# A list scheduler's order: late big loads and independent marked moves in a forgetting-attention and gated-MLP kernel

## The chip, the cores and the metric

One core of one Trainium2 chip. The metric is the device time of one execution in microseconds (us). Besides TensorE (PE), VectorE (DVE), ScalarE (ACT) and GpSimd (POOL), SyncE (SP) issues all of this kernel's DMAs, in one queue, in order.

## The reference

Eight batches of eight heads, 576 positions, head size 64, then one MLP over all 4608 tokens:

```python
scores = (q @ k.T) / sqrt(64)
cum    = cumsum(log(clip(f, 1e-4, 1)))
scores = where(causal, -1e9, scores + cum[:, None] - cum[None, :])
attn   = softmax(scores);  o = attn @ v            # 8 x 8 x 576 x 64
x      = o as [4608, 512]
h      = x @ w_in                                  # 512 -> 2048
g      = h * tanh(softplus(h))                     # Mish
out    = g @ w_out                                 # 2048 -> 512
```

## The kernel before, in words

All operands are split into two float16 halves (high and low), so a product is three matmuls. Two heads are a pair; there are 32 pairs. For a pair `load_qk` (L1047) brings q and k in one transfer of 576 KB into one of two buffers `qk32`; `prep` (L1060) sums their squares on ACT (`junk<-qk`), picks a scale on DVE (`qt`), splits them into `hl`, and issues DMAs into `ST1`: two small copies of cumulated-decay rows from DRAM (`st<-cumd`, 6.8 KB, L1087) and the heads (`st<-hl`); `prep2` (L1094) fills `ST2`. Pairs 1 and 3 use `xa1` in place of `hl`. `load_v` (L980) brings a batch's v in four transfers of 288 KB; `amax_v` sums their squares (`junk<-v`). Then come scores, maxima on DVE (`highest`, a custom instruction that leaves `mn`), exponents on ACT (`st<-b`, `more_e<-b`), their halves `hb`, a transpose by DMA (`pt<-hb`), the products with v (`b<-vv,pt`), normalizing (`x<-b,rr`) and its halves `xp`, transposed into `xa`. The first five pairs go an older way.

The MLP takes 512 tokens at a time (a chunk, 9 in all): products with `w_in` (`b<-xa,wall`), Mish on ACT (`me<-b`), a scaling into halves `gh` and `gl`, products with `w_out` (`b<-gh,wall`, `b<-gl,wall`). Mish and the exponent need different ACT tables, so a change between them is an `ACT_TABLE_LOAD`. Weights come as 32 transfers of 512 KB, are shifted and masked by DVE (`wall<-wall`), summed, scaled and split. The attention of later batches is woven into the MLP of earlier chunks. Chunks 7 and 8 use a scheme with fewer products for part of `w_in`, at the cost of DVE work (sums and differences).

No instruction is issued where the code stands. `Program.choose` (L188) records each operation with its reads and writes, and, where there are several, its possible engines; `deps` (L305) makes dependencies of them; `schedule` (L365) runs `forward` (L478), a list scheduler with a model of the engines and of one DMA queue, and `backward`, which ranks the operations anew, ten times, and keeps one of the ten orders; `emit` (L327, the calls at L333) issues every instruction in that order. The engine of an operation with a choice is picked in `forward` too. The waits that the chip obeys come from the buffers that an instruction really touches, not from this model. `warmed` (L335) puts in matmuls of no use (`b<-idm,idh`) where the model sees PE idle early on.

Two things order transfers among themselves in the model alone. While `nc.mark` is set, each recorded operation also writes an invented region of that name; while `nc.gate` is set, it reads one. `prep` marks the two row copies of pairs 0 to 3 as `rows0` to `rows3`; `load_weights`, the loads of pairs 2 and 3, and the first `load_v` are gated by `rows0`, the next `load_v` by `rows2`. And in `forward` a transfer is taken to have landed at a time worked out from its size:

```python
hw = max(t, hw) + cost[0]
clock[q] = t + 50
dma = max(dma, hw + 650) + cost[1]
end, own = dma + 930 + MARGIN["sync"], 0.0
```

`cost[1]` is the size in bytes over 290, in ns (L272), and t is the model's own time in ns.

Of the kernel before, what the change touches and what calls it, by code (L numbers as in the profile page):

```python
# [27 lines left out]
S = 576  # L28
D = 64
# [100 lines left out]
BACK = 4000  # L130
LOOK = dict(zip(('tensor', 'vector', 'scalar', 'gpsimd', 'sync'), (float(x) for x in ("0", "0", "0", "0", "0",))))
PRIO = 200
MARGIN = dict(tensor=100,vector=100,scalar=100,gpsimd=0,sync=300)
DRAWS = 4
WORK, LAGS, MOVES = 0.02, 50.0, 300.0
F32COL = 8.3
MSW = 97.0
# [23 lines left out]
class Program:  # L161
# [26 lines left out]
    def choose(self, *ways):  # L188

        r, w, opts = [], [], []  # L190
        for way in ways:
            total, port = 0.0, False
            for eng, method, a, kw in way:
                aps = [(k, x) for k, x in list(enumerate(a)) + list(kw.items()) if hasattr(x, "tensor")]
                w += [z for k, x in aps if k in ("out", "accum_out", 0) for z in self.region(x)]
                r += [z for k, x in aps if k not in ("out", "accum_out", 0) for z in self.region(x)]
                if eng == "scalar":
                    (r if method == "activation" else w).append(("table", 0, 1, 0, 1))
                if eng == "tensor":

                    w.append((w[0][0] + "/pe", 0, 1, 0, 1))
                port |= self.shared(eng, method, aps)
                cost = self.cost(eng, method, kw, aps)
                if isinstance(cost, tuple) and total:

                    total = (total[0] + 8, total[1] + cost[1], 0)
                else:
                    total = cost if isinstance(cost, tuple) else total + cost + (80 if total else 0)
            opts.append((eng, way, total, port))
        if self.gate:  # L210
            r.append((self.gate, 0, 1, 0, 1))
        if self.mark:
            w.append((self.mark, 0, 1, 0, 1))
        key = len(self.ops)
        if self.rank is not None:
            key, self.rank[1] = self.rank[0] + self.rank[1], self.rank[1] + self.rank[2]
        self.ops.append((opts, r, w, key))
        self.leads.append(self.lead)
        self.forms.append(self.form(*ways[0][0]) if ways[0][0][0] == "tensor" else None)
        func = ways[0][0][3].get("func") if ways[0][0][0] == "scalar" and len(ways) == 1 else None  # L220
        self.sets.append("mish" if func == AF.Mish else "exp" if func == AF.Exp else None)
        if self.sets[-1] and self.phase is not None:
            n = len(self.sets)
            w.append((f"phase{self.phase}", 0, 1, n, n + 1))
            r.append((f"phase{self.phase - 1}", 0, 1, 0, 1 << 30))

        self.banks.append({
            x.tensor.name for _, _, a, kw in ways[0] for x in list(a) + list(kw.values())
            if hasattr(x, "tensor") and x.space == PSUM})
# [248 lines left out]
    def forward(self, deps, succ, rank):  # L478
# [43 lines left out]
        while len(order) < n:  # L522
            clock["sync"] = max(clock["sync"], hw, dma - BACK)
            best = None
            for q in self.NAMES:
                r, c = ripe[q], coming[q]
# [4 lines left out]
                if r or c:  # L531
                    t = clock[q] if r else max(clock[q], c[0][0])
# [59 lines left out]
            if way[0][1].startswith("dma_start"):  # L592
                hw = max(t, hw) + cost[0]
                clock[q] = t + 50
                dma = max(dma, hw + 650) + cost[1]
                end, own = dma + 930 + MARGIN["sync"], 0.0
            else:
                if q == "tensor":
                    cols, weight, h = cost
# [84 lines left out]
def attn_moe(ctx: ExitStack, tc: tile.TileContext, qk, v, f, w_in, w_out, out):  # L684
# [91 lines left out]
    def flat(t):  # L776
        return t[0:BH].rearrange("p j t s -> p (j t s)")

    tmp = [flat(ST2[i]).bitcast(F32)[:, S * j : S * (j + 1)] for i in (1, 0) for j in range(2)]
    ft = tmp[0]  # L780

    def decay():
        _, on, cm, r1 = tmp
        nc.vector.memset(on, 1.0)
        nc.vector.tensor_scalar(out=ft, in0=ft, scalar1=1e-4, scalar2=1.0, op0=ALU.max, op1=ALU.min)
        nc.scalar.activation(out=ft, in_=ft, func=AF.Ln)
        nc.scalar.preload_act_table_set("exp_and_others")
        nc.vector.tensor_tensor_scan(
            out=cm, data0=on, data1=ft, initial=0.0, op0=ALU.mult, op1=ALU.add)
        c = flat(ST2[1])[:, 0 : 3 * S].rearrange("p (r s) -> p r s", r=3)  # L790
        nc.vector.tensor_scalar(out=c[:, 0], in0=cm, scalar1=8.0, scalar2=None, op0=ALU.mult)
        nc.vector.scalar_tensor_tensor(
            out=r1, in0=cm, scalar=8.0, in1=c[:, 0], op0=ALU.mult, op1=ALU.subtract)
        nc.vector.tensor_copy(out=c[:, 1], in_=r1)
        nc.vector.tensor_tensor(out=c[:, 2], in0=r1, in1=c[:, 1], op=ALU.subtract)
        nc.mark = "sums"
        for h in (slice(0, H), slice(H, BH)):
            nc.mark = None if h.start else "sums"
            nc.sync.dma_start(out=cumd[h], in_=c[h])
        nc.mark = None  # L800
# [259 lines left out]
    def prep(g):  # L1060
# [23 lines left out]
        h0 = b * H + 2 * p  # L1084
        nc.mark = f"rows{g}" if g < NSEL else None
        for t in range(2):
            nc.sync.dma_start(out=ST1[i][D + 3 * t : D + 3 * t + 3, :, t], in_=cumd[h0 : h0 + 2].rearrange("h r s -> r h s"))  # L1087
        nc.mark = None
        for j in range(2):
# [907 lines left out]
```

## Time and profile before

| | |
|---|---|
| median of 3 runs | 1014.1 us (1013.09 to 1015.46) |
| the profiled execution, its own time | 1014.29 us |
| its span on the core | 1012.6 us |
| mean granted TensorE clock | 0.993 |
| PE, DVE, ACT busy, share of the span | 97%, 72%, 72% |
| matmul records, ACT table loads | 7663, 71 |

Nearly all instructions have one line, L333 (the one that issues), so groups are told by the names of the tiles. A PE that is shown busy can still be short of work inside, since matmuls overlap: a matmul of 512 columns is shown with 0.38 us and the next starts 0.22 us after it. "Idle before" is the time in which the engine had nothing running, with what ended it.

### The profile page before, as it was taken

The page shows a single profiled execution, that of the slowest core. Times are in us where ns is not written, and L with a number is a line of the kernel's source. Part 1 is how long each engine was busy: PE and PEld are TensorE (multiplying, and loading weights), DVE is VectorE, ACT ScalarE, POOL GpSimd, SP SyncE. Part 2 cuts the span into 40 slices and gives each one's busy share as a digit, 9 for nine tenths or more (in the row PEclk, how much of TensorE's full clock was granted, in tenths as well). Part 3 has the DMA queues.
Part 4 walks back from the last instruction along what each step waited for, and adds up shares of the span by engine and source line. Part 5 has one row for each costly group of instructions (what it writes and reads, how often), then busy time and mean ns, then how long its engine had stood idle before and what let it go on. Part 6 is the DMA issues. An engine that isn't in the chain of part 4 may idle for free.

```text
span 1012.6 us, 20652 instructions
## 1 busy us (share of the span) xinstructions
PE 978.1 (97%) x7663; PEld 544.1 (54%) x7663; DVE 731.1 (72%) x2002; ACT 728.9 (72%) x1421; POOL 10.4 (1%) x65
## 2 busy tenths in 40 slices
PE   4999899998999999999999999999999999999998
PEld 4788445544554554555455555455555555656664
DVE  7999999986677776776666766776766669953432
ACT  6668999978778777777778877787886665524323
POOL 2000000000000000000000000000000000000000
PEclk8999999999999999999999999999999999999999
DMA  6999974779777857687868766786775432001001
GB/s 198 324 266 244 262 169 108 154 173 187 158 145 160 173 127 153 136 180 145 142 141 179 148 146 142 170 158 115 138 152 112 70 75 72 4 1 42 1 1 42
DMA packets 256446, 139.57 MB, mean 138 GB/s; under 512 B 226650, under 2 KB 227034, under 8 KB 256346
## 3 DMA queue, kind: packets, MB, share of 16 engines
q1 hardware_dynamic: 256346, 138.26, 61.7%
q8 instruction: 60, 0.98, 0.4%
q14 instruction: 40, 0.33, 0.1%
HBM read 45.68 MB, written 9.66 MB: 55 GB/s over the span
## 4 chain that ended last, share of the span: by engine, by line
PE 65%; DVE 16%; ACT 7%; DMA 6%; issue 3%; SPq 1%; POOL 0%; DVEq 0%; ACTq 0%; POOLq 0%
PE b L333 65%; DVE wall L333 3%; DVE b L333 2%; DMA pt<-hb 2%; DMA st<-hl 2%; SPq L333 1%; ACT junk L333 1%; DVE hl L333 1%; DVE hb L333 1%; ACT st L333 1%; ACT hb L333 1%; DMA out_dram<-ot 1%; DVE gl L333 1%; DVE x L333 1%; ACT more_e L333 1%
## 5 line engine op out<-in xcount | busy, mean ns | idle before, releaser
L333 PEld LDWEIGHTS <-wall 128*128 128x128 f16 x3372 | 322.3, 98 | 357.9 <-issue 24.0
L333 PE MATMUL b<-gh,wall 128*128 128x512 f16 x1152 | 366.5, 380 | 0.0
L333 PE MATMUL b<-xa,wall 128*128 128x512 f16 (+1 forms) x1602 | 345.0, 366 | 8.3 <-ACT me L333 4.6
L333 PE MATMUL b<-gl,wall 128*128 128x512 f16 x576 | 218.2, 379 | 0.6 <-DVE gl L333 0.6
L333 PE MATMUL b<-st 70*128 70x512 f16 (+11 forms) x918 | 139.1, 285 | 13.7 <-DMA st<-cumd 6.9
L333 DVE SCALAR_TENSOR_TENSOR gl<-me,gsc,gh 128x512 f16<-128x512 f32 x144 | 106.3, 748 | 32.6 <-ACT gh L333 31.7
L333 ACT ACTIVATE me<-b,cinv 128x512 f32<-128x512 f32 (+1 forms) x130 | 85.0, 660 | 56.6 <-PE b L333 55.7
L333 PEld LDWEIGHTS <-st 70*128 70x128 f16 (+3 forms) x1110 | 87.3, 102 | 63.6 <-issue 18.7
L333 PE MATMUL b<-vv,pt 128*128 128x65 f16 (+5 forms) x2548 | 111.7, 203 | 1.1 <-DMA pt<-hb 0.7
L333 DVE CUSTOM_DVE_ANT_0 b<-b,mskw 128x256 f32<-128x256 f32 (+2 forms) x162 | 91.6, 567 | 9.9 <-PE b L333 8.8
L333 ACT ACT_TABLE_LOAD x70 | 89.8, 1283 | 1.2
L333 PEld LDWEIGHTS <-pt 128*128 128x128 f16 (+1 forms) x2268 | 70.9, 101 | 19.3 <-DMA pt<-hb 2.3
L333 ACT ACTIVATE st<-b,mn 128x512 f32<-128x512 f32 (+3 forms) x120 | 62.1, 548 | 22.7 <-DVE mn L333 19.4
L333 DVE TENSOR_TENSOR hb<-st,hb 128x512 f16<-128x512 f32 x81 | 55.8, 689 | 29.6 <-ACT hb L333 29.1
L333 DVE TENSOR_TENSOR hb<-more_e,hb 128x512 f16<-128x512 f32 x81 | 55.5, 689 | 29.6 <-ACT hb L333 29.3
L333 ACT ACTIVATE more_e<-b,mn 128x512 f32<-128x512 f32 (+3 forms) x123 | 62.4, 539 | 17.3 <-DVE mn L333 15.8
L333 DVE TENSOR_SCALAR gh<-me,gsc 128x512 f16<-128x512 f32 x66 | 31.9, 483 | 45.2 <-ACT me L333 44.3
L333 ACT ACTIVATE gh<-me,gsc 128x512 f16<-128x512 f32 x78 | 55.8, 720 | 1.8
L333 ACT ACTIVATE hb<-more_e 128x512 f16<-128x512 f32 x81 | 50.1, 627 | 9.5 <-DMA pt<-hb 8.8
L333 ACT ACTIVATE hb<-st 128x512 f16<-128x512 f32 x81 | 50.2, 627 | 7.6 <-DMA pt<-hb 5.6
L333 DVE TENSOR_TENSOR me<-b,hb 128x256 f32<-128x256 f32 x42 | 17.5, 422 | 50.5 <-PE b L333 49.9
L333 ACT ACTIVATE junk<-qk 128x576 bf16<-128x576 f32 x60 | 40.8, 680 | 15.5 <-DMA qk<-in_qk_dram 14.8
(173 smaller groups left out, 1005.3 us busy)
## 6 DMA issues: line engine op xcount, KB each, us to landing
st<-hl SPq DMA_DIRECT2D x180, 144.0 KB
qk<-in_qk_dram SPq DMA_DIRECT2D x30, 576.0 KB
v<-in_v_dram SPq DMA_DIRECT2D x32, 288.0 KB
out_dram<-ot SPq DMA_DIRECT2D x36, 256.0 KB
wall<-in_w_in_dram SPq DMA_DIRECT2D x16, 512.0 KB
wall<-in_w_out_dram SPq DMA_DIRECT2D x16, 512.0 KB
pt<-hb SPq DMA_TRANSPOSE x162
st<-xa SPq DMA_DIRECT2D x12, 144.0 KB
```

Source lines behind the costliest of these rows:

```text
L333: r = getattr(real[eng], method)(*a, **kw)
```

## The change

Three edits take effect. A gate reads the whole range of its invented region, and each marked operation writes a byte of its own there, so that marked operations no longer depend on each other, while a gated one still depends on all of them. In `forward`, a transfer whose `cost[1]` is over 1000 ns (the loads of q and k, 2034 ns, of v, 1017 ns, and of weights, 1808 ns) and that is issued after the model's 100 us is taken to land 2500 ns later. `NEAR` is 0, so the branch that it guards is never taken; `splits` only gives a name to a view.

```diff
+NEAR = 0
+LATE = 2500
...
         if self.gate:
-            r.append((self.gate, 0, 1, 0, 1))
+            r.append((self.gate, 0, 1, 0, 1 << 30))
         if self.mark:
-            w.append((self.mark, 0, 1, 0, 1))
+            w.append((self.mark, 0, 1, len(self.ops), len(self.ops) + 1))
...
-                end, own = dma + 930 + MARGIN["sync"], 0.0
+                end, own = dma + 930 + MARGIN["sync"] + LATE * (cost[1] > 1000 and t > 1e5), 0.0
...
         for t in range(2):
+            if g < NEAR:
+                for j in range(2):
+                    nc.sync.dma_start(out=ST1[i][D + 3 * t : D + 3 * t + 3, j, t], in_=splits[h0 + j : h0 + j + 1])
+                continue
             nc.sync.dma_start(out=ST1[i][D + 3 * t : D + 3 * t + 3, :, t], in_=cumd[h0 : h0 + 2].rearrange("h r s -> r h s"))
```

The operations are the same; order and chosen engines differ all over. Three places:

SP, from the heads of pair 0 to those of pair 1 (`st1_0`, `st1_1`, `st1_2` are `ST1` of pairs 0, 1, 2; `cumd` the decay rows; `v32` the v of batch 0). Before:

```order
L333 DMA st1_0_84<-hl_0_114 64x1152 x2
L333 DMA st1_0_84<-cumd_93 3x2x576
L333 DMA st1_1_85<-cumd_93 3x2x576
L333 DMA st1_2_86<-cumd_93 3x2x576
L333 DMA st2_0_87<-hl_0_114 64x1152 x2
L333 DMA st1_0_84<-cumd_93 3x2x576
L333 DMA st2_0_87<-hl_0_114 64x1152 x2
L333 DMA st1_1_85<-cumd_93 3x2x576
L333 DMA st1_1_85<-xa1_91 64x1152
L333 DMA v32_0_115<-in_v_dram 128x576
```

and with the change:

```order
L335 DMA st1_0_84<-hl_0_114 64x1152 x2
L335 DMA st1_0_84<-cumd_93 3x2x576 x2
L335 DMA st1_1_85<-cumd_93 3x2x576 x2
L335 DMA st2_0_87<-hl_0_114 64x1152 x4
L335 DMA v32_0_115<-in_v_dram 128x576
L335 DMA v32_1_116<-in_v_dram 128x576
L335 DMA v32_2_117<-in_v_dram 128x576
L335 DMA v32_3_118<-in_v_dram 128x576
L335 DMA st1_1_85<-xa1_91 64x1152 x2
```

The second row copy of pair 0 moved from the eighth place of the stretch to the fourth, right behind the first; a row copy of pair 2 and a move of pair 1's heads went behind the loads of v.

ACT, up to the exponents of pair 8's middle block (`st1_2_86<-b0_0_130,mn_0_161 128x256`, two of them; `vc_3` are sums of squares of a later batch's v). Before:

```order
L333 ACTIVATE junk_0_112,qa_2_136<-qk32_0_109 128x576 x2
L333 ACTIVATE vv_1_143<-v32_3_118,cols_94 128x9x64
L333 ACTIVATE xp0_0_153<-x32_0_148 128x512
L333 ACT_TABLE_LOAD
L333 ACTIVATE st1_2_86<-b1_0_121,mn_0_161 128x384
L333 ACTIVATE st1_2_86<-b1_0_121,mn_0_161 128x128
L333 ACTIVATE st1_2_86<-b0_0_130,mn_0_161 128x256
L333 ACTIVATE hb_1_175<-st1_2_86 128x512
L333 ACTIVATE st1_2_86<-b0_0_130,mn_0_161 128x256
L333 ACTIVATE junk_0_112,vc_3_199<-v32_0_115 128x576
```

and with the change:

```order
L335 ACTIVATE junk_0_112,vc_3_199<-v32_2_117 128x576
L335 ACTIVATE gh_5_181<-me_0_162,gsc3_103 128x512
L335 ACTIVATE junk_0_112,qa_2_136<-qk32_0_109 128x576
L335 ACTIVATE hl_0_114<-qk32_1_110,qt_1_128 128x576
L335 ACTIVATE vv_1_143<-v32_3_118,cols_94 128x9x64
L335 ACTIVATE xa2_92<-xb_0_193 64x2x64 x2
L335 ACTIVATE x32_0_148<-b0_0_130,rr_3_159 128x64 x4
L335 ACTIVATE xp1_0_154<-x32_0_148 128x128
L335 ACTIVATE xp0_0_153<-x32_0_148 128x512
L335 ACT_TABLE_LOAD
L335 ACTIVATE st1_2_86<-b0_0_130,mn_0_161 128x256 x2
```

Three of the squares of v (the third is the first row) and other attention work now stand ahead of these exponents instead of behind them.

ACT, up to the first reader of the load of pair 11's q and k (`junk_0_112,qa_3_151<-qk32_1_110`). Before:

```order
L333 ACTIVATE gh_8_190<-me_3_172,gsc3_103 128x512
L333 ACTIVATE xp1_0_154<-x32_0_148 128x128
L333 ACTIVATE xa2_92<-xb_0_193 64x2x64
L333 ACTIVATE me_4_176<-b3_0_124,cinv3_99 128x512
L333 ACTIVATE xa2_92<-xb_0_193 64x2x64
L333 ACTIVATE gh_9_194<-me_4_176,gsc3_103 128x512
L333 ACTIVATE junk_0_112,qa_3_151<-qk32_1_110 128x576
L333 ACT_TABLE_LOAD
L333 ACTIVATE st1_2_86<-b0_0_130,mn_1_185 128x512
```

and with the change:

```order
L335 ACTIVATE hb_1_175<-more_e_105 128x512
L335 ACTIVATE hv_0_179<-evs_81 128x128
L335 ACTIVATE junk_0_112,vc_3_199<-v32_3_118 128x576
L335 ACTIVATE xa2_92<-xb_0_193 64x2x64
L335 ACTIVATE more_e_105<-b1_0_121,mn_0_161 128x512
L335 ACTIVATE st1_2_86<-b0_0_130,mn_0_161 128x384
L335 ACTIVATE hb_0_168<-more_e_105 128x512
L335 ACTIVATE st1_2_86<-b0_0_130,mn_0_161 128x128
L335 ACT_TABLE_LOAD
L335 ACTIVATE me_1_165<-b2_0_123,cinv3_99 128x512
L335 ACTIVATE junk_0_112,qa_3_151<-qk32_1_110 128x576
```

The reader now comes behind one Mish (`me_1`) of its phase where it came behind four, and its load moved further still: 12 ACT instructions are issued between the load and this reader, where there were 5.

## Rows read from the trace of the kernel before

**Rows 1.** The page's head: the span and section 1, busy time by engine.

```profile
span 1012.6 us, 20652 instructions
...
PE 978.1 (97%) x7663; PEld 544.1 (54%) x7663; DVE 731.1 (72%) x2002; ACT 728.9 (72%) x1421; POOL 10.4 (1%) x65
```

**Rows 2.** Busy time by stage: stretch in us, its length, then busy us (and instructions) of PE, PEld, DVE, ACT and POOL, the granted clock, the DMA share and GB/s.

```profile
125.00:150.00 25.00, 25.00 (x188) 12.38 (x184) 24.54 (x70) 24.17 (x39) 0.14 (x1) 1.00 0.69 165
150.00:175.00 25.00, 24.27 (x200) 12.85 (x199) 24.58 (x70) 24.41 (x54) 0.14 (x1) 1.00 0.56 114
175.00:200.00 25.00, 24.65 (x192) 12.44 (x191) 24.97 (x73) 24.75 (x43) 0.28 (x1) 1.00 0.65 137
...
225.00:250.00 25.00, 21.89 (x167) 11.03 (x165) 18.63 (x61) 19.29 (x41) 0.14 (x1) 1.00 0.90 197
...
270.00:850.00 580.00, 575.75 (x4546) 293.50 (x4545) 403.53 (x1121) 443.09 (x856) 2.77 (x20) 1.00 0.69 140
```

**Rows 3.** The timeline of PE at some places: start and length in us, instruction, and in brackets the idle time before it and what ended that.

```profile
18.51 0.27 PE L333 MATMUL b<-st 128*128 128x128 f16 x1 [6.94 <-DMA st<-cumd]
...
201.20 0.38 PE L333 MATMUL b<-gl,wall 128*128 128x512 f16 x1
201.42 0.38 PE L333 MATMUL b<-gh,wall 128*128 128x512 f16 x1
201.85 0.60 PE L333 MATMUL b<-st 70*128 70x256 f16 x4
...
237.56 0.59 PE L333 MATMUL b<-st 70*128 70x512 f16 x2 [1.48 <-ACT more_e L333]
...
242.06 5.34 PE L333 MATMUL b<-xa,wall 128*128 128x512 f16 x24 [1.63 <-ACT st L333]
...
402.74 5.34 PE L333 MATMUL b<-xa,wall 128*128 128x512 f16 x24 [0.90 <-ACT st L333]
```

**Rows 4.** The timeline of SP's issues, 13 to 23 us.

```profile
14.22 1.05 SPq L333 DMA_DIRECT2D st<-cumd  x3
15.37 1.12 SPq L333 DMA_DIRECT2D st<-hl  x2
16.53 0.46 SPq L333 DMA_DIRECT2D st<-cumd  x1
...
18.96 0.46 SPq L333 DMA_DIRECT2D st<-cumd  x1
19.53 0.46 SPq L333 DMA_DIRECT2D st<-xa  x1
20.03 2.03 SPq L333 DMA_DIRECT2D v<-in_v_dram  x4
```

**Rows 5.** The timeline of DVE at the start and at 201 us.

```profile
19.56 1.35 DVE L333 TENSOR_REDUCE mx<-b 128x4 f32<-128x512 f32 x3 [1.36 <-PE b L333]
...
28.08 0.16 DVE L333 TENSOR_REDUCE am_m<-vc 128x1 f32<-128x4 f32 x1 [1.38 <-ACT junk L333]
...
32.45 0.42 DVE L333 TENSOR_SCALAR wall<-wall 128x512 int32<-128x512 int32 x1
...
201.11 0.42 DVE L333 TENSOR_TENSOR x<-b,rr 128x256 f32<-128x256 f32 x1
201.45 0.35 DVE L333 TENSOR_SCALAR x<-b,rr 128x128 f32<-128x128 f32 x1
```

**Rows 6.** Groups of instructions, different shapes apart: count, then busy us and mean ns of one, then idle time before them and what ended it.

```profile
L333 DVE SCALAR_TENSOR_TENSOR gl<-me,gsc,gh 128x512 f16<-128x512 f32 x144 | 106.3, 748 | 32.6 <-ACT gh L333 31.7
L333 DVE TENSOR_TENSOR hb<-st,hb 128x512 f16<-128x512 f32 x81 | 55.8, 689 | 29.6 <-ACT hb L333 29.1
L333 DVE SCALAR_TENSOR_TENSOR hl<-qk,qt,hl 128x576 f16<-128x576 f32 x58 | 46.1, 810 | 4.6 <-ACT hl L333 2.3 <-ACT me L333 1.2 <-DMA st<-hl 0.7
L333 DVE CUSTOM_DVE_ANT_0 b<-b,mskw 128x384 f32<-128x384 f32 x54 | 30.4, 563 | 3.2 <-PE b L333 2.9
L333 DVE SCALAR_TENSOR_TENSOR vv<-v,cols,vv 128x576 f16<-128x576 f32 x27 | 22.0, 814 | 0.9 <-ACT vv L333 0.9
L333 DVE TENSOR_SCALAR hl<-qk,qt 128x576 f16<-128x576 f32 x21 | 10.7, 515 | 12.1 <-DMA st<-hl 12.1
L333 DVE TENSOR_SCALAR qt<-qt 128x1 int32<-128x1 int32 x64 | 9.3, 149 | 0.9
L333 DVE CAST xp<-x 128x128 f16<-128x128 f32 x6 | 1.3, 223 | 0.0
...
L333 ACT ACT_TABLE_LOAD x70 | 89.8, 1283 | 1.2
L333 ACT ACTIVATE junk<-v 128x576 bf16<-128x576 f32 x32 | 22.0, 689 | 3.5 <-DMA v<-in_v_dram 3.3
```

**Rows 7.** The timeline of ACT where it waited longest for loads of q and k, and at 394 us.

```profile
229.21 0.68 ACT L333 ACTIVATE junk<-qk 128x576 bf16<-128x576 f32 x1 [3.97 <-DMA qk<-in_qk_dram]
...
235.14 0.68 ACT L333 ACTIVATE junk<-qk 128x576 bf16<-128x576 f32 x1 [0.81 <-DMA qk<-in_qk_dram]
...
393.96 0.68 ACT L333 ACTIVATE junk<-qk 128x576 bf16<-128x576 f32 x1 [0.54 <-DMA qk<-in_qk_dram]
```

**Rows 8.** The timeline of SP: the issues of the two loads that end the first two waits of Rows 7.

```profile
223.87 0.59 SPq L333 DMA_DIRECT2D qk<-in_qk_dram  x1
...
229.53 0.56 SPq L333 DMA_DIRECT2D qk<-in_qk_dram  x1
```

More of the change, by code (lines that the diff above doesn't have):

```diff
@@ L780, in attn_moe @@
     ft = tmp[0]
+    splits = flat(ST2[1])[:, 0 : 3 * S].rearrange("p (r s) -> p r s", r=3)
     def decay():
@@ L789, in decay @@
             out=cm, data0=on, data1=ft, initial=0.0, op0=ALU.mult, op1=ALU.add)
-        c = flat(ST2[1])[:, 0 : 3 * S].rearrange("p (r s) -> p r s", r=3)
+        c = splits
         nc.vector.tensor_scalar(out=c[:, 0], in0=cm, scalar1=8.0, scalar2=None, op0=ALU.mult)
```

## The prediction

> **What bounds the kernel now.** I read the page's head first, then the stages, then the idle time of PE, then what the engines behind that idle time waited for. PE is busy 97% of the span, DVE and ACT 72% each [rows 1], but the share is a mean over unlike stages. By stage there are three [rows 2]. From 125 to 200 us all three engines are full: PE 73.9, DVE 74.1 and ACT 73.3 of 75 us. There whatever stands too early in the order of DVE or ACT delays something that PE needs. From 225 to 250 us PE loses 3.1 us, with DVE and ACT at 19 of 25. From 270 to 850 us PE is idle for 4.25 us in all (580 less 575.75), while DVE and ACT have a quarter and more to spare: PE alone sets the pace, and an order of the others can only win or lose those 4 us. The single gaps of PE [rows 3] say who is late: at 18.51 us a copy of decay rows, at 237.56 and 242.06 us the exponents of ACT (1.48 and 1.63 us), at 402.74 us another one (0.90 us).
>
> The later two follow from loads of q and k. ACT stood at a square of such a load from 225.24 to 229.21 us and again for 0.81 us before 235.14 [rows 7], with everything behind these squares held, since ACT works in order. Ten us later PE runs out of exponents. The load at fault was issued at 223.87 us and its reader began at 229.21 us, 5.3 us later; the next one at 229.53 and 235.14, 5.6 us [rows 7, 8]. The third, of 0.54 us at 393.96, stands 9 us before the gap at 402.74 [rows 3, 7].
>
> **The change, part by part.** The operations are the same 10,533, so products cost what they cost; the order has one matmul of no use more (0.22 us at most by the spacing of wide products [rows 3]) and two ACT table loads more, 1.283 us each [rows 6], which matter only where ACT is full (below). Everything else is position and choice of engine.
>
> *Marks: the start.* The first real product waits for the second row copy of pair 0, issued at 16.53 us as the eighth DMA behind the heads [rows 3, 4]. It is now the second of that stretch, so it leaves 14.22 plus a third of 1.05, at about 14.6 us, 1.9 us sooner, and the product can start so much sooner. Less of it reaches the next stage. DVE gets to its first weight at 32.45 us, after a wait of 1.38 us for the squares of v at 28.08 [rows 5]; the loads of v are issued from 20.03 us, and ahead of them now stand two issues fewer (one row copy and one move from `xa1`, 0.46 us each [rows 4]), 0.9 us. I take **-0.8 us** for the point at which DVE starts on weights; the ends are 0 (the transfers are served at the same rate, so v lands as before) and -1.9 (all of the first product's lead).
>
> *The full stage.* Take as a mark the four products of 256 columns of pair 8's middle block, at 201.85 us [rows 3]: PE began them 0.3 us after DVE had ended the normalizing at 201.53 that frees their bank [rows 3, 5], so they came as soon as DVE let them. I counted what each engine must do ahead of the second of them in the two orders. PE: 9 more products of 512 columns (201 in place of 192) at 0.216 us from one to the next [rows 3], 1.9 us. DVE: 23 more instructions. Four first splits of q or k (4 x 0.515), two rests of them (2 x 0.810), four narrow halves of x (4 x 0.223), one each of `gl`, a rest of `hb`, a rest of v and a 384 wide maximum (0.748 + 0.689 + 0.814 + 0.563), nine of one or a few columns (9 x 0.149 [all rows 6]) come to 8.7 us; a wide half of x and a narrow maximum more, and two normalizations fewer, cancel within 0.2. An instruction on DVE starts about 0.08 us before the one ahead ends (201.45 against 201.53 [rows 5]), so 23 of them overlap by 1.8: **6.9 us** more. ACT: 7 more, of which five are squares (0.689 each and about as much as 0.1 for reading the sum), and two more table loads (2 x 1.283 [rows 6]): 6.5 us, and the remainder, copies and exponents against fewer halves of q, k and x, near +0.5: 7.0 us. So the mark comes 6.9 - 0.8 later by DVE's clock, of which PE has used 1.9 for work that it would have done later: **+4.2 us**. The ends: 0, if DVE's surplus lies where it was going to idle, and +4.3 from ACT (7.0 - 0.8 - 1.9), which gives nearly the same; without the gain at the start it is +5.1. I take the value from DVE, since the mark's own wait is on DVE. What is borrowed is given back: some 35 us of products further on, DVE's count ahead is within 1.3 us of before again. But PE is full meanwhile, and does not catch up.
>
> *Late loads.* Between the load of pair 11 and its first square ACT now has 12 instructions and not 5, some 5.6 us of work at 0.6 us or less each, as long as the 5.3 us that the load takes [rows 7, 8]. Between the next load and its square 10 stand in place of 6. So I take the 3.97 us wait as gone, and with it PE's idle 1.48 + 1.63: **-3.1 us**, between 0 (another wait takes its place, since ACT carries the same work) and -3.1. At 393.96 us the load had 2 ACT instructions to hide behind and has 11; the 0.90 us at 402.74 goes: **-0.9**, between 0 and -0.9. In most later pairs the reader moves back by 1 to 6 ACT instructions; those waits had no gap of PE behind them and I cost them at nothing: PE's own work covers them from 270 us on. If that cover is gone in places, all of the remaining 3 us idle there could double; I keep 1.5 us either way.
>
> A rule that speaks against this part: the Trainium skill, "DMA: Bandwidth & Descriptors", Anatomy of one DMA, fits a transfer on the gpsimd path with a fixed 2.0 us and the bytes at 436 GB/s. For 576 KB that is an estimate of 3.4 us, on another path than SP's; by it the load would have landed at 227.2 us, nearly half of ACT's wait would be due to something else, and the third term would be about -1.6 and the sum 1015.7 us. The measured 5.3 and 5.6 us decide against it.
>
> **Sum.** +4.2 - 3.1 - 0.9 = +0.2 us on the profiled execution's own 1014.29 us (1.7 us around its span of 1012.6). The median of the runs is 0.2 us lower, 1014.1. So I expect a median of **1014.3 us**: no change that can be told. About 0.2%, 2 us, is what a measurement of this kernel can tell from none; the three runs lie within 2.4.
>
> **The rivals.**
>
> *DVE's surplus costs nothing: faster.* The extra instructions stand ahead of the mark in DVE's order, but if DVE and ACT now idle less in the first 100 us (ACT is not full there) or the products behind are not needed so soon, PE keeps its pace, and only gains are left: -0.8 - 3.1 - 0.9 = -4.8, **1009.5 us**. For it: by the end of the stage the counts agree again, and PE has 9 wide products more in hand. Against it: 0.3 us of slack at the mark, and DVE at 74.1 of 75 us.
>
> *The late loads only move the wait: slower.* ACT carries two more table loads and five more squares into the stage in which it is full. It then comes to 225 us behind as before, late by its own work and not by a load, and PE idles for the same exponents. The delay of the mark stays whole: +4.2, **1018.5 us**. It decides itself from PE's idle time between 215 and 260 us on: above 2 us it is this rival. For it: the order puts the loads, and with them the squares, earlier against PE's work. Against it: ACT had 5.7 us of 25 to spare at 225 to 250 us [rows 2].
>
> *The change does not do what it says.* The chip knows neither marks nor the 2.5 us; all that reaches it is order. The orders differ from the eighth DMA on, so this can only mean that differences cancel, which is the forecast's own result.
>
> **How the numbers follow.** The forecast (both effects, within 2 us) has 0.42, faster 0.32, slower 0.26: two separate gains are read from rows directly, so the faster case gets a little more than the slower one. The range takes in both rivals, 1009.5 and 1018.5, with half a us beyond the faster for the start's other 1.1 us: 1009.0 to 1018.5. The forecast's own range is 1012.3 to 1016.3.
>
> **What would show it.** The first real product near 16.6 us in place of 18.51, and the first weight on DVE near 31.6. The four 256 wide products of pair 8 near 208 us, 9 wide products further on in PE's count. No wait of ACT for q and k over 1 us between 200 and 260 us, and PE idle under 1 us there. ACT's waits for q and k, over the span, well below before's. Two more table loads. I am wrong if PE's mark comes at 204 us or sooner (then the first rival), or if PE loses more than 2 us between 215 and 260 (then the second), or if the stage from 270 to 850 us, where I see nothing to win, moves by more than 1.5 us.

## The result and the profile after: 1.1% slower

Median 1024.75 us (1023.44 to 1026.79, 4 runs) against 1013.6 us of before beside it: ratio 1.0109, 95% interval 1.0086 to 1.0132. The forecast was 1014.3, the range ended at 1018.5. Two further measurements gave 1.0088 [1.0057, 1.0118] and 1.0098 [1.0067, 1.0129] (below). Runs of one kernel on the later chips are up to 1% apart (before: 1012.37 to 1023.62 us in 35 runs), so times are compared only as ratios with their intervals, and places in profiles beside them.

The page's head, to be held against [rows 1]:

```profile
span 1023.4 us, 20673 instructions
...
PE 981.7 (96%) x7664; PEld 545.4 (53%) x7664; DVE 735.1 (72%) x2011; ACT 728.1 (71%) x1428; POOL 9.3 (1%) x65
```

The span is 10.8 us longer. PE idles 41.7 us (1023.4 less 981.7) in place of 34.5, which is 7.2 of it; the other 3.6 are a longer busy time for the same matmuls, in part at a lower clock (below). By stage (columns as in [rows 2]):

```profile
0.00:100.00 100.00, 84.81 (x929) 71.63 (x929) 91.16 (x253) 73.14 (x171) 5.52 (x39) 0.95 0.89 256
100.00:125.00 25.00, 18.54 (x130) 10.10 (x129) 24.97 (x84) 24.11 (x43) 0.36 (x1) 0.93 1.09 274
125.00:200.00 75.00, 69.11 (x490) 33.95 (x487) 71.33 (x209) 69.48 (x127) 0.28 (x2) 0.98 0.65 144
200.00:270.00 70.00, 68.84 (x543) 34.93 (x542) 54.91 (x161) 54.69 (x111) 0.42 (x3) 1.00 0.72 161
270.00:850.00 580.00, 572.70 (x4487) 290.35 (x4484) 400.23 (x1112) 439.08 (x861) 2.77 (x20) 1.00 0.70 140
```

PE's idle time, length less busy, before and after: 16.3 and 15.2 up to 100 us; 4.0 and 6.5 to 125; 1.1 and 5.9 to 200; 3.2 and 1.2 to 270; 4.3 and 7.3 to 850. So there are two losses (100 to 200 and 270 to 850 us), one gain of 2 us where the gaps of [rows 3] at 237 and 242 us were, and 1.1 us at the start that is no gain (below). From 125 to 200 us DVE and ACT lost 2.8 and 3.9 us as well (71.33 and 69.48 where [rows 2] add up to 74.1 and 73.3): all three engines have more waits there than before.

PE's timeline there, and the four products of pair 8 that were the prediction's mark:

```profile
185.18 4.26 PE L335 MATMUL b<-xa,wall 128*128 128x512 f16 x19 [1.41 <-ACT me L335]
192.97 0.48 PE L335 MATMUL b<-wsc,ones 128*128 128x6 f32 x2 [1.97 <-DVE wsc L335]
...
212.16 0.61 PE L335 MATMUL b<-st 70*128 70x256 f16 x4
```

The mark comes at 212.16 and not at 208. What the engines did from the start up to it, before and with the change (columns as in [rows 2]):

```profile
0.00:201.85 201.85, 180.43 (x1636) 120.03 (x1636) 192.95 (x546) 170.37 (x345) 7.36 (x43) 0.97 0.83 216
```
```profile
0.00:212.16 212.16, 184.61 (x1645) 121.97 (x1646) 199.39 (x574) 178.03 (x364) 6.30 (x43) 0.96 0.80 208
```

DVE worked 6.4 us more and stood idle 3.9 us more (length less busy: 12.8 in place of 8.9); 2.9 of the 3.9 lie behind 100 us, where two waits for exponents of ACT were the largest part (us in all, times, longest):

```profile
DVE b L335 <- ACT more_e L335: 2.6, 2, 1.6
```

PE had 9 products more, as counted. In two further profiles of the change (e7 and e16 below) the mark comes at 214.63 and 211.78 us with the same 199.4 us of DVE's work.

The wait for `wsc` is that for the last weight: its sum of squares stands before the `gh` and `gl` products of the first chunk. SP's loads of the last two weights, DVE's shifts (`wall<-wall`) and the scale's first step on DVE (`wsc<-wsq`):

```profile
167.66 0.37 SPq L335 DMA_DIRECT2D wall<-in_w_out_dram  x1
179.24 0.36 SPq L335 DMA_DIRECT2D wall<-in_w_out_dram  x1
```
```profile
186.72 0.42 DVE L335 TENSOR_SCALAR wall<-wall 128x512 int32<-128x512 int32 x1
188.97 0.68 DVE L335 SCALAR_TENSOR_TENSOR wall<-wall 128x512 int32<-128x512 int32 x1
190.23 0.68 DVE L335 SCALAR_TENSOR_TENSOR wall<-wall 128x512 int32<-128x512 int32 x1
192.75 0.16 DVE L335 TENSOR_SCALAR wsc<-wsq 128x6 f32<-128x6 f32 x1
```

Before issued the last of these loads at 167.01 us and began its sum on PE at 176.78. The raw buffers explain a part of the 12 us between the two loads. Four of the last five weights pass one after another through one buffer, each load waiting for DVE's shift of the weight before it, so in the planner's model LATE adds up along them: counted in the order, the last two loads moved from 84.6 and 92.5 us of products to 89.8 and 99.1, and the last sum from 100.8 to 110.4. The load's own 6.6 us of products are about half of its 12 us; the rest is that PE came later to the same place.

Behind 270 us ACT no longer waits for q and k at all. In before it did, from 270 to 850 us (us in all, times, longest):

```profile
ACT junk L333 <- DMA qk<-in_qk_dram: 9.1, 8, 2.4
```

Yet PE idles 3 us more. The largest of what it waited for there in the change, the same columns:

```profile
PE b L335 <- ACT me L335: 2.4, 6, 0.6
PE b L335 <- ACT more_e L335: 1.9, 4, 0.9
PE b L335 <- DMA pt<-hb: 1.1, 4, 0.4
```

### The profile page after: what moved, and what is told of

Same layout as the page of the kernel before. It is cut to its first block, busy times and chain, and to the rows that moved or that the text cites. A ratio compares the mean times of both kernels' runs of the same rounds, so it can differ in the third digit from the quotient of the medians.

```text
span 1023.4 us, 20673 instructions
## 1 busy us (share of the span) xinstructions
PE 981.7 (96%) x7664; PEld 545.4 (53%) x7664; DVE 735.1 (72%) x2011; ACT 728.1 (71%) x1428; POOL 9.3 (1%) x65
## 4 chain that ended last, share of the span: by engine, by line
PE 59%; DVE 16%; ACT 12%; DMA 7%; issue 4%; SPq 1%; ACTq 0%; DVEq 0%
PE b L335 59%; DMA pt<-hb 4%; DVE wall L335 3%; ACT L335 2%; DVE b L335 2%; DMA st<-hl 2%; DVE hl L335 2%; ACT hb L335 2%; ACT junk L335 2%; ACT st L335 1%; DVE gl L335 1%; DVE hb L335 1%; ACT more_e L335 1%; ACT me L335 1%; SPq L335 1%
## 5 line engine op out<-in xcount | busy, mean ns | idle before, releaser
L335 PE MATMUL b<-st 70*128 70x512 f16 (+10 forms) x918 | 140.5, 287 | 13.0 <-DMA st<-cumd 9.6
L335 ACT ACTIVATE hb<-more_e 128x512 f16<-128x512 f32 x81 | 50.3, 626 | 10.3 <-DMA pt<-hb 7.5
L335 DVE SCALAR_TENSOR_TENSOR hl<-qk,qt,hl 128x576 f16<-128x576 f32 x58 | 46.0, 809 | 4.9 <-ACT hl L335 2.6
```

The source lines that it names most:

```text
L335: r = getattr(real[eng], method)(*a, **kw)
```

## The experiments

Five groups, each timed on one chip beside before (whose median there was 1014.1 to 1016.5 us). Idle is PE's, and in the last column DVE's, in us, from each kernel's one profile: stretch less busy. LATE "on weights" means that loads of weights of the model's 100 to 200 us get it.

| kernel | median, us | ratio to before | idle 100-125 | 125-200 | 200-270 | 270-850 | DVE 100-200 |
|---|---|---|---|---|---|---|---|
| before | | | 4.0 | 1.1 | 3.2 | 4.3 | 1.0 |
| the change | 1024.75 | 1.0109 | 6.5 | 5.9 | 1.2 | 7.3 | 3.7 |
| e1 marks alone | 1021.30 | 1.0047 [1.0025, 1.0068] | 3.9 | 3.5 | 2.2 | 5.8 | 3.8 |
| e2 LATE alone | 1019.34 | 1.0025 [1.0003, 1.0047] | 3.8 | 4.4 | 0.0 | 5.6 | 1.4 |
| e3 LATE after 200 | 1014.00 | 0.9971 [0.9948, 0.9993] | 4.6 | 0.6 | 1.2 | 5.7 | 0.2 |
| e4 LATE 100 to 200 | 1018.43 | 1.0004 [0.9981, 1.0027] | 5.7 | 4.9 | 0.9 | 4.7 | 0.4 |
| e5 LATE, not on weights | 1019.23 | 1.0026 [1.0004, 1.0049] | 4.1 | 3.2 | 2.2 | 6.0 | 3.5 |
| e6 LATE on weights alone | 1017.16 | 0.9994 [0.9974, 1.0014] | 4.2 | 5.2 | 1.6 | 3.9 | 0.5 |
| e7 the change again | 1027.06 | 1.0088 [1.0057, 1.0118] | 7.1 | 5.7 | 2.1 | 7.6 | 5.1 |
| e8 before, redrawn | 1017.83 | 1.0013 [0.9992, 1.0035] | 2.1 | 2.7 | 2.8 | 4.2 | 2.3 |
| e9 LATE 200 to 270 | 1012.06 | 0.9958 [0.9935, 0.9980] | 4.5 | 0.6 | 1.5 | 5.9 | 0.2 |
| e10 v after 200 | 1012.01 | 0.9966 [0.9948, 0.9985] | 4.5 | 0.6 | 2.1 | 5.3 | 0.2 |
| e11 q, k after 200 | 1016.28 | 1.0006 [0.9983, 1.0028] | 4.5 | 1.0 | 3.2 | 5.5 | 0.2 |
| e12 as e3 | 1013.20 | 0.9973 [0.9954, 0.9992] | 3.3 | 0.9 | 2.1 | 5.3 | 0.4 |
| e13 last weights put back | 1024.16 | 1.0076 [1.0049, 1.0103] | 6.2 | 5.7 | 1.1 | 6.6 | 3.5 |
| e14 LATE 100 to 270 | 1019.20 | 1.0040 [1.0020, 1.0060] | 4.6 | 5.1 | 1.2 | 3.2 | 3.4 |
| e15 e13 and e14 | 1019.06 | 1.0033 [1.0015, 1.0050] | 6.3 | 7.1 | 2.1 | 2.8 | 1.7 |
| e16 the change again | 1026.15 | 1.0098 [1.0067, 1.0129] | 5.5 | 6.2 | 1.7 | 8.3 | 3.6 |

The last column sorts the times better than any one column of PE's: the seven kernels in which DVE idles 0.5 us or less (e3, e4, e6, e9 to e12) have ratios of 0.9958 to 1.0006, and all with more of it than before has, 1.4 us and up, have 1.0013 to 1.0109. No run moved this idle time by itself, so that it sets the time is likely and not shown.

**Which edit, and where: e1 to e4.** Edits to the changed kernel; e2 takes both lines on marks back to those of before.

```diff
-LATE = 2500                                    # e1
+LATE = 0
-    + LATE * (cost[1] > 1000 and t > 1e5)      # e3
+    + LATE * (cost[1] > 1000 and t > 2e5)
+    + LATE * (cost[1] > 1000 and 1e5 < t < 2e5)   # e4
```

> The two edits on marks alone, LATE = 0. In the order the last weight loads stand 6 to 11 us of products sooner than before (PE work 73.6 and 86.2 us ahead of them, before 84.6 and 92.5), and from 260 us of products on the order is that of before almost everywhere. Late-load theory (the change's loss comes from LATE: about +7 us up to 260 us, by weights that come later in the order, and about +4 us behind that, by another order of ACT): nothing is lost here but a redraw of the start, 1011 to 1016 us, PE idle from 270 to 850 us as before (about 4 us). Mark theory (the loss up to 260 us comes from the new order of the start): about 1020 us, and the stage behind 270 us as before. Any-redraw theory (the order of before was a lucky one, every other order of the first 200 us loses several us): 1018 to 1022 us.

> LATE = 2500 alone, marks as before. The last two weight loads stand at 90.2 and 99.1 us of products, as in the whole change (89.8 and 99.1; before 84.6 and 92.5), and from 260 us of products on the order is that of the whole change almost everywhere. Late-load theory: the whole loss is here, 1021 to 1026 us, with a PE stall of 3 to 5 us about 175 to 200 us at the last weight (b<-wsc,ones waits for DVE) and about 7 us of PE idle from 270 to 850 us. Mark theory: only the part behind 260 us, about 1017.5 us. Any-redraw theory: 1020 to 1026 us.

> Marks as in the change, LATE only for transfers that the model issues after 200 us (t > 2e5). The last weight loads stand at 76.5 and 86.5 us of products (before 84.6 and 92.5); from 260 us of products on the order is that of the whole change almost everywhere. Late-load theory: only the later part of the loss, +3 to +4 us: 1016 to 1018 us, PE idle from 270 to 850 us about 7 us as in the whole change. Mark theory: both parts, 1022 to 1025 us. Any-redraw theory: 1022 to 1026 us.

> Marks as in the change, LATE only for transfers that the model issues between 100 and 200 us. The last two weight loads stand at 90.0 and 99.3 us of products, as in the whole change; from 260 us of products on the order is that of before almost everywhere. Late-load theory: the first part of the loss alone, about +7 us: 1018 to 1022 us, with a stall at the last weight near 190 us, PE idle from 270 to 850 us about 4 us as before. Mark theory: about the same time, 1020 us, so it is told apart by the kernel with marks alone. Any-redraw theory: 1018 to 1022 us.

The late-load theory missed e1 (1021 for 1011 to 1016) and e3 (a gain, where it had said a loss); its idle time came right in place: 4.4 and 4.9 us from 125 to 200 with LATE in the model's 100 to 200 us, 0.6 without in e3, but 3.5 in e1. e2 came 1.7 us under its range (1019.34 for 1021 to 1026), with 5.6 us of idle time behind 270 us where about 7 was expected; e4 lies inside (1018.43 for 1018 to 1022). The time of e1 is what the other two theories had said, but both had e3 lose as well. Marks alone can lose several us too, and the parts do not add up to the whole. In e1's profile PE's idle time is only 2.6 us above before's (37.1 and 34.5 over the whole span); its busy time is 4.6 us longer (982.7 and 978.1), so idle time alone does not give the time.

**Weights, or q and k, or any redraw: e5 to e8.** The condition on `cost[1]` is narrowed to q, k and v (e5) or to weights (e6); e8 is before with a random number of 0 to 2 places added to each first rank.

```diff
+    + LATE * (cost[1] > 1000 and not 1900 > cost[1] > 1100 and t > 1e5)   # e5
+    + LATE * (1900 > cost[1] > 1100 and t > 1e5)                          # e6
-NZ = 0                                                                    # e8
+NZ = 2
```

> Marks as in the change, LATE for the loads of q, k and v only, none for weights. The last four weight loads share one raw buffer, each waiting for DVE's shift of the one before, so LATE on weights adds up along them; here it is gone: the last two loads stand at 81.1 and 92.5 us of products and the last sum of weights at 103.4 (before 84.6, 92.5, 100.8; the whole change 89.8, 99.1, 110.4). Weight-chain theory (the stall of 150 to 200 us comes from LATE on this chain): PE idle from 150 to 200 us at most 1.5 us, as in the kernels without LATE there (0.2 and 0.9; before 1.1), no gap of PE over 1 us between 215 and 260 us; the time 1013 to 1018 us, with what the redraw does to 75 to 130 us still open. LATE-on-q-and-k theory (the stall comes from the squares of q, k and v that ACT meets elsewhere): idle of 3.5 to 5.5 us there as in the three kernels with LATE, 1018 to 1022 us. Any-redraw theory: any value, 1016 to 1022 us.

> Marks as in the change, LATE for the loads of weights only. The last two loads stand at 89.8 and 98.7 us of products, the last sum of weights at 108.5; from 260 us of products on the order is that of before almost everywhere. Weight-chain theory: PE idle from 150 to 200 us 3.5 to 5.5 us, and the two gaps at 237 and 242 us of before, which LATE on q and k removes, come back (1.5 us or more of PE idle from 225 to 250 us): 1018 to 1024 us. LATE-on-q-and-k theory: idle 150 to 200 us under 1.5 us, 1013 to 1017 us. Any-redraw theory: 1016 to 1022 us.

> The changed kernel itself, beside the others and the same runs of before. All theories: 8 to 11 us over before; with the same places as in its first profile, PE idle about 12 us from 100 to 200 us, of it about 5 from 150 to 200, and about 7 us from 270 to 850 us. A tail of 5.5 us or less there, as the two other kernels with nearly the same order from 260 us of products on had it, says that some 1.5 us of the first profile's 7.3 were that run's own.

> The kernel before, with NZ = 2 and SEED = 1: a random number of 0 to 2 places is added to each operation's first rank, nothing else; the order differs from that of before all over, no weight comes later (83.8 and 92.2 us of products for the last two loads, 103.3 for the last sum). Any-redraw theory (before is a lucky order, whatever differs loses): 1018 to 1024 us, PE idle from 100 to 200 us of 7 us or more. Weight-chain theory: 1012 to 1019 us, PE idle from 150 to 200 us at most 1.5 us, the gaps at 225 to 250 us present in some form (2 us or more), since no load is put later.

The idle time from 125 to 200 us sorts the kernels: 4.4 to 7.1 in all nine profiles with LATE on weights, 0.6 to 3.5 in all nine without. So PE's idle time there goes with LATE on weights, though e5 and e8 had more of it from 150 to 200 us (2.4 and 1.6) than the at most 1.5 expected. The time does not go with it: e6, with 5.2 us of this idle time, takes as long as before (1017.16 us, where the weight-chain theory had 1018 to 1024), and e5, with 3.2, takes longer (1019.23 for 1013 to 1018). LATE on weights alone is therefore not what costs the change its 1%. One plain redraw costs nothing that could be told. e7, and later e16, repeat the places of the loss; their 7.6 and 8.3 us behind 270 us say that the first profile's 7.3 was not that run's own.

**The same early order, four endings: e9 to e12.** e9 is e3 with LATE only up to the model's 270 us; e10 is e3 with loads of v alone, e11 with q and k alone.

```diff
+    + LATE * (cost[1] > 1000 and 2.7e5 > t > 2e5)          # e9
+    + LATE * (1100 > cost[1] > 1000 and t > 2e5)           # e10
+    + LATE * (cost[1] > 1900 and t > 2e5)                  # e11
```

> As the kernel with LATE after 200 us only, but LATE ends where the model's time passes 270 us. Its order is the same as that one's up to about 200 us of products, word for word, and from 260 us of products on that of before almost everywhere. Tail theory (the order that LATE makes behind 270 us costs PE 2 to 3 us, though it takes ACT's waits for q and k away): PE idle from 270 to 850 us 4 to 5 us, against 5.7 of the kernel with LATE after 200 us; ACT waits there for q and k again 8 us or more; 1 to 3 us faster than that kernel, the two gaps near 237 and 242 us still gone. Theory that the tails only differ from run to run: the same time within 1 us as that kernel beside it.

> As the kernel with LATE after 200 us only, but for loads of v alone; the order is the same up to about 140 us of products. Theory that LATE on q and k closes the two gaps near 237 and 242 us: they come back, PE idle from 225 to 250 us 2 to 3 us and ACT waits for q and k there over 3 us; 2 to 4 us slower than the kernel beside it with LATE on all loads after 200 us. Theory that the marks or the redraw closed them: PE idle there under 1 us, the same time.

> As the kernel with LATE after 200 us only, but for loads of q and k alone; the order is the same up to about 140 us of products. Theory that LATE on q and k closes the gaps: PE idle from 225 to 250 us under 1 us, as with LATE on all; the same time as the kernel beside it within 2 us, the tail being a third order.

> The kernel with LATE after 200 us only once more, beside the three that differ from it in one condition. All theories: 2 to 3 us under before, as before, PE idle from 150 to 200 us 0.2 us, from 225 to 250 us under 0.5, from 270 to 850 us about 5.7.

With one order up to 140 us of products the idle time from 125 to 200 us is 0.6, 0.6, 1.0 and 0.9 us: there the order decides, not the run. The theory that LATE on q and k closes the gaps fell. e11, with it, has no wait of ACT for them from 200 to 270 us and still idles as much as before; e10, without it, waits 0.5 us and idles less. From 200 to 270 us, e10 and then e11:

```profile
200.00:270.00 70.00, 67.93 (x496) 33.60 (x493) 53.50 (x165) 58.26 (x120) 0.28 (x2) 1.00 0.87 182
```
```profile
200.00:270.00 70.00, 66.78 (x486) 32.91 (x485) 57.10 (x177) 52.40 (x112) 0.28 (x2) 1.00 0.82 176
```

What ended PE's gaps in e11 was a transpose by DMA (1.3 us), the normalizing on DVE (1.2) and Mish (0.7). The one gap of e10 between 215 and 260 us stands some 8 us behind its one wait for q and k, as the prediction read it in before:

```profile
238.16 5.34 PE L335 MATMUL b<-xa,wall 128*128 128x512 f16 x24 [1.22 <-ACT st L335]
```
```profile
229.61 0.68 ACT L335 ACTIVATE junk<-qk 128x576 bf16<-128x576 f32 x1 [0.53 <-DMA qk<-in_qk_dram]
```

So a late load may still make a gap; taking the wait away does not take the gaps away. The tail theory missed as well: e9 idles 5.9 us behind 270 us, as much as e3 and e12, though its order there is nearly that of before. e9 and e10 are the fastest kernels here, 0.4 and 0.3% under before, faster than both kernels of this study; what makes them so beyond the low idle time of that early order is not taken apart.

**Undoing parts inside the change's own order: e13 to e16.** In e13 the schedule of the change is computed as it is and then 25 operations of the last weights are put at the number of matmuls ahead that they have in before; dependencies kept. e14 ends LATE at the model's 270 us, e15 does both.

```diff
+TO = {910: 925, 911: 948, 912: 977, 915: 987, ..., 942: 1109, ..., 970: 1147}   # e13
-        return best[1:]
+        return self.moved(deps, best[1]), best[2]
...
+        for i, n in TO.items():
+            key[i] = (n, *key[i][1:])
...
+    + LATE * (cost[1] > 1000 and 2.7e5 > t > 1e5)                              # e14
```

> The changed kernel's own order, with 25 operations put back to where they stand in the order of before (by the number of matmuls ahead): the last two weight loads, the shifts of the weights around them, two squares, the last sum of weights and the small operations on it. All other operations keep their order and their engines. Weight-chain theory: the stall at the last weight goes (PE idle from 175 to 200 us under 1.5 us, where the change has 4.0 and 3.8), 3 to 5 us faster than the change beside it: 1022 to 1024 us if that is at 1027. Theory that the stall is DVE's surplus and only shows at the last weight: the same time within 1 us, PE waits for other DVE operations instead, 140 to 200 us.

> The whole change, but LATE ends where the model's time passes 270 us. The order up to 260 us of products is nearly that of the change (mean shift 0.3 us or less but for 60 to 140 us of products, 1.2 and 0.5), behind it that of before almost everywhere. Tail theory (the later order costs 3 us): 2.5 to 3.5 us faster than the change beside it, PE idle from 270 to 850 us under 5.5 us where the change has 7.3 and 7.5. Theory that the tail's loss is what PE hands on from the stage before: the same time within 1 us, idle about 7. Between them, as the pair of kernels with LATE after 200 us and from 200 to 270 us had it: 1 us.

> Both: LATE ends at the model's 270 us, and the same 25 operations of the last weights put back to where before has them. If the two causes add up: the gain of the hoisted kernel plus that of the one with LATE up to 270 us, 4 to 8 us under the change, 1019 to 1023 us if that is at 1027.

> The changed kernel beside the three that undo parts of it. All theories: 8 to 11 us over before; PE idle from 100 to 200 us 12 to 13.5 us, from 270 to 850 us 7 to 7.6.

The weight-chain theory in its narrow form fell: e13 has its last load at 170.31 us and its sum 9 us sooner than the change, but PE waits there as well, DVE's and ACT's idle time stays, and the mark of pair 8 comes at 213.25 us, among the change's three. 1.0076 against 1.0098, with overlapping intervals, is no gain that can be told.

```profile
183.66 0.39 PE L336 MATMUL b<-wsc,ones 128*128 128x6 f32 x2 [1.76 <-DVE wsc L336]
```
```profile
125.00:200.00 75.00, 69.28 (x508) 34.16 (x507) 71.49 (x204) 69.20 (x125) 0.28 (x2) 0.98 0.62 139
```

e14 is the clear one: with the early order of the change nearly kept, the later order of before gives back 4 to 5 us of idle time behind 270 us, while ACT waits again for q and k. Its stage and those waits:

```profile
270.00:850.00 580.00, 576.80 (x4550) 293.00 (x4548) 404.47 (x1127) 443.83 (x862) 2.78 (x20) 1.00 0.69 140
```
```profile
ACT junk L335 <- DMA qk<-in_qk_dram: 8.9, 7, 2.2
```

Behind six of these seven waits of ACT no gap of PE follows within ten us; behind the one of 0.78 us at 399.32 comes a gap of 0.90 at 408.11. So most of the 9 us cost PE nothing, and the order that avoids them costs some 4. e15 says the same beside e13 (2.8 for 6.6). With another early order there is no such gain: e9, with the later order of before, idles 5.9 us there, e3 and e12, with that of the change, 5.7 and 5.3. How the cost hangs on what comes in from the stage before is open.

**Which engine's order: e17 and e18.** As e13, but with `TO` holding 220 operations of DVE, or 112 of ACT, all that both orders have between 50 and 140 us of products on that engine.

> The changed kernel's order, in which 220 DVE operations that stand between 50 and 140 us of products in both orders are put where before has them; those of ACT and PE keep their order but for what they have to follow, and all keep their engines. Theory of DVE's surplus (the prediction's own: what stands too early on DVE delays PE): most of the 6 to 9 us of the stretch from 100 to 200 us come back, 1018 to 1021 us, PE idle from 100 to 200 us under 8 us where the change has 12 to 13. Theory that it is ACT's order (table loads and Mish against exponents): under 2 us back, 1024 to 1027 us. Theory that the two engines' orders must only fit each other: slower than the change, over 1027 us.

> The same with 112 ACT operations in place of those of DVE. Theory of DVE's surplus: under 2 us back, 1024 to 1027 us. ACT's order: 1018 to 1021 us, PE idle from 100 to 200 us under 8 us. Theory that the orders must fit each other: slower than the change, over 1027 us.

1079.18 us (1.0647 [1.0626, 1.0668]) and 1055.21 us (1.0405 [1.0387, 1.0423]): 53 and 29 us more than the change took on another chip (1026.15), for putting one engine's operations where the better kernel has them. From 200 to 225 us, e17 and e18:

```profile
200.00:225.00 25.00, 13.96 (x74) 6.44 (x75) 13.63 (x36) 12.71 (x25) 0.00 (x0) 0.73 0.47 105
```
```profile
200.00:225.00 25.00, 17.39 (x71) 7.42 (x72) 13.34 (x42) 13.81 (x25) 0.00 (x0) 0.66 0.49 98
```

All three engines idle for a third to a half of the time. The orders of the engines have to fit each other, as the third theory said. What DVE's surplus costs by itself these two runs cannot tell, since the misfit covers it.

## Why the prediction was wrong

**The start, -0.8.** The first product came at 15.21 us, sooner than the 16.6 forecast (the row copies left together at 13.17). The loads of v left at 17.03, 3.0 us sooner, and DVE's wait for their squares ended at 27.23 in place of 28.08, 0.85 sooner, as the term said. But the first weight on DVE came at 33.31 and not at 31.6: more maxima (`mx<-b`) and short waits now stand between those squares and the first weight (6.1 us from one to the other in place of 4.4), and PE waited 4.81 us for pair 1. The row copy that its row names had long been issued; the last heads of pair 1 (`st<-xa`) now go behind all four loads of v:

```profile
13.17 1.36 SPq L335 DMA_DIRECT2D st<-cumd  x4
14.58 2.40 SPq L335 DMA_DIRECT2D st<-hl  x4
17.03 2.83 SPq L335 DMA_DIRECT2D v<-in_v_dram  x4
19.97 1.11 SPq L335 DMA_DIRECT2D st<-xa  x2
```

```profile
27.02 0.27 PE L335 MATMUL b<-st 128*128 128x128 f16 x1 [4.81 <-DMA st<-cumd]
```
```profile
27.23 0.16 DVE L335 TENSOR_REDUCE am_m<-vc 128x1 f32<-128x4 f32 x1 [4.65 <-ACT junk L335]
...
33.31 0.41 DVE L335 TENSOR_SCALAR wall<-wall 128x512 int32<-128x512 int32 x1
```

Up to 100 us PE idled 1.1 us less than before (15.2 and 16.3), but the same order idled 16.0 and 14.2 us in e7 and e16, so this is no gain that can be told.

**The full stage, +4.2: the step that failed.** The sign and the place were right, the size by half: the mark came 10.3 us later, 1.9 of it for the nine products, so +8.4 (10.8 and 8.0 in e7 and e16). The count itself was good: 6.4 us more work on DVE for the 6.9 forecast, 7.7 on ACT for 7.0. What failed is that the sum let DVE do this work without any more waiting, and from a start 0.8 us sooner. DVE idled 3.9 us more up to the mark (6.3 and 3.5 in e7 and e16), of it 2.9 in the stage that was read as full: 6.4 + 3.9 - 1.9 = 8.4. Why these orders make DVE wait stays open. "Late loads" was also costed for q and k alone, though the change's own list has the weights in it; the nine profiles with LATE on weights are those in which PE idles 4.4 us and more from 125 to 200 us, but e6 shows that this alone costs no time, and e13 that the last weights' places are not what delays the mark. On top, PE's busy time up to the mark is 2.2 us longer than the nine products make it. Some of that is clock: a gap can be followed by the lower clock, as the wait at 192.97 us was, behind which the granted clock was 0.60 on average (in e16 it was 1.00 behind the same wait):

```profile
193.90:197.20 3.30, 3.23 (x10) 1.20 (x10) 3.30 (x14) 1.91 (x3) 0.00 (x0) 0.60 0.83 206
```

**Late loads, -3.1 and -0.9.** ACT's waits for q and k went entirely, and PE's idle time from 215 to 260 us fell from 3.1 to 1.2 us (1.6 and 1.7 in e7 and e16), so the second rival's mechanism did not come and 2.0 of the 3.1 did. But e11 shows that the link, a load that is late and a gap ten us later, is not enough to price it: there the waits are gone and PE idles 2.3 us in the same stretch, for other things. The estimate of about -1.6 for this term, worked out in the prediction from the Trainium skill, "DMA: Bandwidth & Descriptors", Anatomy of one DMA, lies nearer by number, but no run here shows its share; the nearness may be luck. The 0.90 us at 402.74 went, and others came.

**270 to 850 us, "nothing to win", ±1.5: the second step that failed.** PE idled 3.0 to 4.0 us more there (7.3, 7.6 and 8.3 for 4.3), against a term of nothing; it was one of the prediction's own signs of being wrong. That most of ACT's waits there cost nothing was right (e14); what was not asked is what the order gives up to avoid them.

**The sum.** Up to the mark +8.4 came for +4.2, and behind it +2.4 for -4.0 (10.8 of span less 8.4): there PE idled 1.1 us more in all, and its busy time grew by some 1.4 us, a term that the sum did not have. The third rival's point, that only order reaches the chip, was true, and its conclusion that differences cancel was not. The rival on the slower side was nearest in time with another mechanism.

## What to carry to other kernels

A change to a planner's costs is a change to every engine's order: list everything its condition catches (here the weights, in a chain through one buffer, where a delay adds up) before pricing the case it was meant for. When all engines are full, a count of the work ahead of a mark gives only that part of a delay which is work: here it was right within 0.5 us, and the waits that the new order added, 3.9 us, were missing. Widen the range to the spread of the planner's other orders of the same operations, here 1012 to 1027 us. A wait of an engine that has slack is no loss by itself: look first whether anything behind it was late.

## What the runs showed of the hardware

The same kernel in the same order came to the same products within 0.1 us up to 108 us in two profiles, and then the clock fell at different gaps. The change (first) and its repetition e7 (second), two stretches each; the number behind that of POOL is the granted clock, 0.50 being 1.2 GHz and 1.00 being 2.4:

```profile
108.44:111.20 2.76, 2.76 (x7) 1.01 (x7) 2.76 (x8) 2.75 (x6) 0.00 (x0) 0.50 1.06 314
115.20:120.20 5.00, 3.82 (x24) 1.91 (x23) 5.00 (x22) 4.94 (x8) 0.00 (x0) 1.00 1.05 249
```
```profile
108.44:111.20 2.76, 1.87 (x11) 0.73 (x11) 2.76 (x8) 2.73 (x6) 0.00 (x0) 1.00 1.06 284
115.20:120.20 5.00, 5.00 (x14) 1.83 (x14) 4.10 (x19) 4.94 (x8) 0.00 (x0) 0.50 1.06 274
```

PE's first products in these stretches, with the gaps:

```profile
108.44 3.02 PE L335 MATMUL b<-xa,wall 128*128 128x512 f16 x7 [2.14 <-ACT me L335]
115.05 0.27 PE L335 MATMUL b<-idm,idh 128*128 128x128 f16 x2 [1.92 <-DVE wsc L335]
115.16 2.75 PE L335 MATMUL b<-xa,wall 128*128 128x512 f16 x12
```
```profile
108.49 1.67 PE L335 MATMUL b<-xa,wall 128*128 128x512 f16 x7 [2.14 <-ACT me L335]
115.10 0.37 PE L335 MATMUL b<-idm,idh 128*128 128x128 f16 x2 [2.27 <-DVE wsc L335]
115.27 5.32 PE L335 MATMUL b<-xa,wall 128*128 128x512 f16 x12
```

In the first the clock was low behind a gap of 2.14 us and at full behind the next, of 1.92; in the second full behind the same 2.14 us and low behind 2.27. The same twelve products took 2.75 us in one and 5.32 in the other. So what a gap of about 2 us costs differs from run to run. The runs of before are spread over 11 us (35 runs) with a mean clock of 0.987 to 0.997, those of e3 over 2.6 us (12 runs) with 0.992 to 0.995; why e3's are closer is not shown.
